# The value loads of a cached attention step, begun by ScalarE on its own DMA queue

## The chip, the cores and the metric

The kernel runs on one core of one Trainium2 chip. The metric is the device time of one execution in microseconds (us); lower is better. Before the change it is 1310.84 us, the median of three runs (1310.8 to 1311.07).

## The reference

One decode step: attention over a long cache, beside a gated feed-forward net, mixed by a gate per row. All data are float32.

```python
# x (4, 1, 512); k_cache, v_cache (4, 32, 4096, 128); wq (512, 4096); wo (4096, 512)
# w_gate, w_up (512, 1792); w_down (1792, 512); gate_w (512)
g = sigmoid((x * gate_w).sum(-1, keepdims=True))
q = (x @ wq) split into 32 heads of 128
p = softmax(einsum("bhqd,bhkd->bhqk", q, k_cache) * 128 ** -0.5)
o = einsum("bhqk,bhkd->bhqd", p, v_cache)
a = o (heads joined) @ wo
b = (gelu(x @ w_gate) * (x @ w_up)) @ w_down
out = g * a + (1 - g) * b
```

The two caches are 268 MB each, so nearly all that is moved is read once and used for very little arithmetic.

## The kernel before, in words

The 128 pairs of batch row and head are done in 32 tiles (NT). A tile holds four heads (HT) of one batch row: tile i is head group i // 4 and batch row i % 4 (`heads`, L128). Its keys lie as 128 partitions of 16384 numbers: each head takes 32 partitions, each partition 128 consecutive positions of 128 numbers, a row of 64 KB in memory. The values lie the same way. So one load of keys (K) or of values (V) is 128 rows of 64 KB, 8.39 MB.

There are two buffers for keys, K[0] and K[1], by the tile's parity, and one for values, V. At the start V holds wq, and at the end K[0] and K[1] hold the weights of the feed-forward net and wo.

What a tile passes through:

- **VectorE** (`keys`, L293): waits for the keys in memory and for the query in QB, multiplies the keys by the query in place (L303), sums over the 128 numbers (L304), then raises `k_free` (L305), which frees the key buffer. Then the maximum of the scores (L306 to L308), which is handed to ScalarE. VectorE's loop (L334) does the keys of tile i+1 and then divides tile i (`divide`, L310: L311 and L312), for which it waits for TensorE's `turn` of tile i. It runs in order: a division that waits holds the keys of tile i+2 behind it.
- **ScalarE** (`beside`, L322): copies the next query from PSUM (L235), spreads the one after (L229), computes the exponentials of the scores (`weights`, L318), waits for TensorE's values, and copies their sum from PSUM to o (L331).
- **TensorE** (loop at L267): spreads the next query (L232), sums the weights (`totals`, L238), waits for the values in V, multiplies weights by values in 64 matmul instructions (`values`, L245), and after ScalarE's copy of o turns it (`turn`, L250). The first of the turn's matmuls raises TensorE's count, which `at_tile[i]` names: from there on V is known to be free.

Nearly all loads are begun by SyncE (SP), in an order that is written out (L348 to L365): for each tile it waits until the keys of tile i are done and begins the keys of tile i+2, then waits for `at_tile[i]` and begins the values of tile i+1. At the end it begins w_gate and w_up, the values of tile 31, then w_down and wo; the last pieces of wo (L391) follow when the net's hidden row is done. All of these stand on one queue. ScalarE's own queue carries two small loads at the start, x and gate_w (L147 and L149).

After tile 30 TensorE does the two matmul groups of the net (L284); after tile 31 the output of the attention and of the net go through w_down and wo together (`project`, L411, and L466), and the result is stored.

Of the kernel before, what the change touches and what calls it, by code (L numbers as in the profile page):

```python
# [34 lines left out]
def tile_gated_mix(ctx: ExitStack, tc: tile.TileContext, x, kc, vc, wq, wo, w_gate, w_up, w_down, gate_w, out):  # L35
    nc = tc.nc
    P = 128
    B, H, S, D = kc.shape
# [3 lines left out]
    HT = 4  # L42
    PH = P // HT
    R = S // PH
    TW = R * D
    NG = H // HT
    NT = NG * B
# [34 lines left out]
    V = kv.tile([P, TW], F32, name="v")  # L82
# [25 lines left out]
    def semaphore(name):  # L108
        counters.append(ctx.enter_context(nc.semaphore(name)))
        return counters[-1]  # L110

    ctx.enter_context(tc.tile_critical(sync_engine=mybir.EngineType.SP, no_gpsimd_drain=True))
    SP = Line(nc.sync, None)
# [8 lines left out]
    def take(engine, sem, n=1):  # L122
        engine.wait_ge(sem, n).then_inc(sem, -n)  # L123

    sem_k = [semaphore(f"sem_k{s}") for s in range(2)]
    sem_v = semaphore("sem_v")

    def heads(src, i):  # L128
        g, b = divmod(i, B)
        return src[b, HT * g:HT * g + HT].rearrange("h (p r) d -> (h p) (r d)", p=PH)  # L130

    def load(dst, src, sem=None, name=None, engine=nc.sync):
        sem = sem or semaphore(name)
        engine.dma_start(dst, src).then_inc(sem, 16)  # L134
        return sem, 16

    def load_k(i):
        load(K[i % 2], heads(kc, i), sem_k[i % 2])

    def load_v(i):  # L140
        load(V, heads(vc, i), sem_v)

    HC, HW = KC // 2, TW // 2
    wq_rows = wq.rearrange("(p c) n -> p (c n)", c=KC)
# [68 lines left out]
    for s in range(2):  # L213
# [3 lines left out]
        wq_done = PE.do(u)  # L217
# [10 lines left out]
    def spread_query(pair, s):  # L228
        return nc.scalar.activation(QX, tile_of(QT, pair, s)[:, :, None].to_broadcast([P, HT, PH]), AF.Copy)  # L229
# [4 lines left out]
    def take_query(s):  # L234
        nc.scalar.activation(QB[s], qp[:, :D], AF.Copy, scale=scale).then_inc(a_to_d, 1)  # L235
# [25 lines left out]
    L1 = NT - 1  # L261
    PE.wait(have_QX, have_picks, have_zeros)
    at_tile = [(PE.sem, PE.n + i + 1) for i in range(NT)]
# [50 lines left out]
    def weights(s):  # L314
        take(nc.scalar, d_to_a)
        for h in range(HT):
            q = slice(h * PH, (h + 1) * PH)
            t = nc.scalar.activation(PM[q, :, h], SC[s][q, :], AF.Exp, bias=NM[s][q, :], scale=1.0,  # L318
                                     accum_out=RS[q, h:h + 1])
        return t  # L320

    def beside(s, following):  # L322
        take(nc.scalar, p_to_a)
        take_query(1 - s)
        if following is None:
            nc.scalar.sem_inc(a_to_p, 1)
        else:
            spread_query(following, s).then_inc(a_to_p, 1)
        weights(s).then_inc(a_to_p, 1)
        take(nc.scalar, p_to_a)  # L330
        nc.scalar.activation(o, po, AF.Copy).then_inc(a_to_p, 1)  # L331

    keys(0, got_k0)
# [6 lines left out]
    take(nc.vector, p_to_d)  # L340
    divide(NT // 2 - 1, 0).then_inc(d_to_p, 1)

    with nc.scalar.Fori(1, NT // 2) as i:
        for s in range(2):
            beside(s, i)
    beside(0, None)

    SP.wait(wq_done)  # L348
    load_v(0)
    for i in range(NT - 2):  # L350
        SP.wait((k_free, i + 1))
        load_k(i + 2)
        SP.wait(at_tile[i])
        load_v(i + 1)

    wo_rows = wo.rearrange("(p i) n -> p (i n)", i=WR)
    SP.wait((k_free, NT - 1))
    for s, a in enumerate((w_gate, w_up)):
        load(f[:, s * KC * F:(s + 1) * KC * F], a.rearrange("(p c) n -> p (c n)", c=KC), sem_up[s])
    SP.wait(at_tile[L1 - 1])  # L360
    load_v(L1)
    SP.wait((k_free, NT))
    got_down = load(down[:, :DR * DM], w_down.rearrange("(p i) n -> p (i n)", i=DR), name="got_down")
    got_wo = [load(down[:, (DR + r0) * DM:(DR + r1) * DM], wo_rows[:, r0 * DM:r1 * DM], name=f"got_wo{r0}")
# [90 lines left out]
    i = W2  # L455
# [42 lines left out]
```

## Time and profile before

| | |
|---|---|
| median of three runs | 1310.84 us |
| the profiled execution | 1310.84 us, its span 1309.1 us |
| busy: VectorE, TensorE matmul, ScalarE | 87%, 30%, 8% |
| moved from HBM | 564.67 MB, 431 GB/s over the span |
| DMA queue of SyncE (q1) | 564.67 MB |
| DMA queue of ScalarE (q10) | 0.02 MB |
| mean granted TensorE clock | 0.635 of full speed |

In rows of the profile PE is TensorE, DVE VectorE, ACT ScalarE, SP SyncE; SPq and ACTq are the sequencers that begin a DMA, and the time in such a row is that of beginning it, not of the transfer. A row of the timeline gives start, duration, engine, line, operation, what is written and read, shape and count, and in brackets how long the engine was idle before it and what ended that. "DVEq L123" there means that the engine's own sequencer stood in a wait of `take` (L122). A row of the windows gives the stretch, its length, each engine's busy time with the count of instructions, the granted clock, the share of time in which the DMA engines were busy, and GB/s.

### The profile page before, as it was taken

What the parts mean: (1) busy time and instruction counts of PE and PEld (TensorE: products, weight loads), DVE (VectorE), ACT (ScalarE), POOL (GpSimd) and SP (SyncE); (2) the same over time, 40 slices, a digit from 0 to 9 for tenths busy, and PEclk for the clock granted to TensorE, in tenths of its full rate; (3) what the DMA queues carried; (4) which work ended last, traced back from release to release, by engine and by line L of the source; (5) the groups of instructions that cost most, each with busy time, mean ns of one, the idle gap of its engine ahead of it and who ended that gap; (6) DMA issues with size and microseconds to landing.
All of it is one profiled execution on the core that took longest, in us unless ns stands there. A gap on an engine that the chain in (4) does not pass through costs nothing. (4 is left out here: it accounts for less than half of the span.)

```text
span 1309.1 us, 6991 instructions
## 1 busy us (share of the span) xinstructions
PE 389.2 (30%) x2708; PEld 134.3 (10%) x2708; DVE 1144.8 (87%) x267; ACT 108.5 (8%) x360; POOL 0.7 (0%) x6
## 2 busy tenths in 40 slices
PE   4032113333212333312333321233331133332147
PEld 1010001101001111000111100111110011110012
DVE  1999999899899989989998998989999898998950
ACT  1010000000000000000000000000000000000010
POOL 0000000000000000000000000000000000000000
PEclk9565566666566666556666655666665666665589
DMA  9999999999999999999999999999999999999998
GB/s 401 433 446 421 445 431 439 443 423 443 423 443 423 445 429 437 447 423 443 423 443 423 445 427 439 441 429 443 423 443 423 443 423 445 435 435 443 412 438 359
DMA packets 11130, 564.76 MB, mean 431 GB/s; under 512 B 1244, under 2 KB 1260, under 8 KB 1652
## 3 DMA queue, kind: packets, MB, share of 16 engines
q1 hardware_dynamic: 11108, 564.67, 99.6%
q8 instruction: 3, 0.05, 0.0%
q10 hardware_dynamic: 16, 0.02, 0.0%
q14 instruction: 3, 0.02, 0.0%
HBM read 564.67 MB, written 0.01 MB: 431 GB/s over the span
## 5 line engine op out<-in xcount | busy, mean ns | idle before, releaser
L303 DVE TENSOR_TENSOR k<-k,QB 128x16384 f32<-128x16384 f32 (+1 forms) x33 | 551.4, 16708 | 64.6 <-DVEq L123 61.9
L304 DVE TENSOR_REDUCE SC<-k 128x128 f32<-128x16384 f32 x32 | 551.0, 17220 | 4.7
L245 PE MATMUL bank<-v,PM 128*16 128x512 f32 x2048 | 291.8, 734 | 568.7 <-PEq L123 568.7
L245 PEld LDWEIGHTS bank<-v,PM 128*16 128x16 f32 x2048 | 69.0, 112 | 764.8 <-issue 764.8
L238 PE MATMUL bank<-RS,ones 128*128 128x4 f32 x64 | 17.7, 348 | 294.4 <-PEq L123 294.4
L331 ACT ACTIVATE o<-bank 128x512 f32<-128x512 f32 x31 | 18.5, 597 | 872.3 <-ACTq L123 872.3
L318 ACT ACTIVATE PM<-SC,nm 32x128 f32<-32x128 f32 x128 | 65.9, 515 | 195.4 <-ACTq L123 193.9
L238 PEld LDWEIGHTS bank<-RS,ones 128*128 128x128 f32 x64 | 15.9, 308 | 299.6 <-issue 299.6
L250 PE MATMUL bank<-pick,o 128*128 128x4 f32 x256 | 32.8, 251 | 28.7 <-PEq L123 28.7
L250 PEld LDWEIGHTS bank<-pick,o 128*128 128x128 f32 x256 | 31.0, 191 | 57.3 <-issue 57.3
L311 DVE RECIPROCAL ri<-bank 128x4 f32<-128x4 f32 x32 | 5.8, 183 | 22.0 <-DVEq L123 22.0
L318 ACT ACTIVATION_READ_ACCUMULATOR PM<-SC,nm 32x1 f32 x128 | 25.0, 195 | 0.0
L220 DVE COPY QT<-bank 128x16 f32<-128x16 f32 x8 | 0.9, 179 | 18.5 <-PE bank L216 18.5
L232 PE MATMUL bank<-ident,QX 128*128 128x128 f32 x66 | 15.4, 316 | 1.6 <-ACT QX L229 1.6
L306 DVE TENSOR_REDUCE m<-SC 128x1 f32<-128x128 f32 x32 | 9.2, 286 | 7.6 <-DVEq L123 7.6
L204 PE MATMUL bank<-v,xT 128*32 128x512 f32 x64 | 11.6, 892 | 5.8 <-DMA v<-in_A_wq 5.8
L235 ACT ACTIVATE QB<-bank 128x128 f32<-128x128 f32 x32 | 8.9, 277 | 50.3 <-ACTq L123 49.7
L312 DVE TENSOR_TENSOR OT<-bank,ri 128x4 f32 (+1 forms) x32 | 5.2, 161 | 7.5 <-DVEq L123 7.2
L307 DVE STREAM_TRANSPOSE mt<-m 128x32 f32<-128x32 f32 x32 | 6.8, 211 | 4.7
L470 DVE COPY res<-bank 128x128 f32<-128x128 f32 x1 | 0.3, 292 | 11.9 <-PE bank L466 11.9
L232 PEld LDWEIGHTS bank<-ident,QX 128*128 128x128 f32 x66 | 10.0, 191 | 2.8 <-issue 1.6
L308 DVE TENSOR_REDUCE nm<-mt 128x1 f32<-128x32 f32 x32 | 6.0, 186 | 4.8 <-DVEq L123 2.3
(57 smaller groups left out, 61.5 us busy)
## 6 DMA issues: line engine op xcount, KB each, us to landing
v<-in_A_wq SPq DMA_DIRECT2D x2, 4096.0 KB, 16.9
k<-in_A_k_cache SPq DMA_DIRECT2D x2, 4096.0 KB, 35.3
k<-in_B_w_gate SPq DMA_DIRECT2D x1, 3584.0 KB, 31.3
k<-in_B_w_up SPq DMA_DIRECT2D x1, 3584.0 KB, 39.4
k<-in_B_w_down SPq DMA_DIRECT2D x1, 3584.0 KB, 29.0
k<-in_A_wo SPq DMA_DIRECT2D x1, 2560.0 KB, 34.8
k<-in_A_wo SPq DMA_DIRECT2D x1, 2048.0 KB, 39.2
k<-in_A_wo SPq DMA_DIRECT2D x1, 1536.0 KB, 33.6
```

The costliest lines, as they stand in the source:

```text
L204: t = nc.tensor.matmul(PO[s][32 * j:32 * j + 32], xT[:, c, :], w[:, c, n0:n0 + HB * D], start=c == 0, stop=c == KC - 1)
L232: return nc.tensor.matmul(qp[:, :D], QX.rearrange("p h k -> p (h k)"), ident, start=True, stop=True)
L235: nc.scalar.activation(QB[s], qp[:, :D], AF.Copy, scale=scale).then_inc(a_to_d, 1)
L238: return nc.tensor.matmul(tot, ones, RS, start=True, stop=True)
L245: t = nc.tensor.matmul(po[32 * c:32 * c + M], p[:, j * M:(j + 1) * M], V[:, j * RJ * D:(j + 1) * RJ * D], start=j < 4, stop=j >= n - 4)
L250: return [nc.tensor.matmul(quo, o[:, j * D:(j + 1) * D], pick[:, j, :], start=j == 0, stop=j == RJ - 1) for j in range(RJ)]
L303: then(nc.vector.tensor_tensor(part, part, QB[s][:, None, :].to_broadcast([P, n, D]), op=OP.mult))
L304: then(nc.vector.tensor_reduce(SC[s], k, axis=AX.X, op=OP.add))
L306: then(nc.vector.tensor_reduce(m1, SC[s], axis=AX.X, op=OP.max))
L307: then(nc.vector.transpose(mt, m1.to_broadcast([P, 32])))
L318: t = nc.scalar.activation(PM[q, :, h], SC[s][q, :], AF.Exp, bias=NM[s][q, :], scale=1.0, accum_out=RS[q, h:h + 1])
L331: nc.scalar.activation(o, po, AF.Copy).then_inc(a_to_p, 1)
```

## The change

SyncE no longer begins values. ScalarE begins all 32 loads of values, on its own queue, with the same rows of 64 KB: V of tile 0 ahead of its loop, and V of the next tile in each `beside`, right behind the wait for TensorE's values and ahead of the copy of o. SyncE keeps keys and weights, in the order they had, with only the waits for free key buffers. The address of a value load now comes from the loop's register g, the batch row b being fixed in the code; so ScalarE's loop does four tiles in a turn (one head group) instead of two, and the last three tiles of that kind are written out.

```diff
-    def load_v(i):
-        load(V, heads(vc, i), sem_v)
-
...
-    def beside(s, following):
+    def load_values(g, b):
+        rows = vc[b, bass.ds(g * HT, HT)].rearrange("h (p r) d -> (h p) (r d)", p=PH)
+        load(V, rows, sem_v, engine=nc.scalar)
+
+    def beside(s, following, g, b):
         take(nc.scalar, p_to_a)
...
         weights(s).then_inc(a_to_p, 1)
         take(nc.scalar, p_to_a)
+        load_values(g, b)
         nc.scalar.activation(o, po, AF.Copy).then_inc(a_to_p, 1)
...
-    with nc.scalar.Fori(1, NT // 2) as i:
-        for s in range(2):
-            beside(s, i)
-    beside(0, None)
-
-    SP.wait(wq_done)
-    load_v(0)
+    load_values(0, 0)
+    with nc.scalar.Fori(0, NG - 1) as g:
+        for b in range(B):
+            beside(b % 2, 2 * g + 1 + b // 2, g + (b + 1) // B, (b + 1) % B)
+    for b in range(B - 1):
+        beside(b % 2, NT // 2 - 1 if b < 2 else None, NG - 1, b + 1)
+
     for i in range(NT - 2):
         SP.wait((k_free, i + 1))
         load_k(i + 2)
-        SP.wait(at_tile[i])
-        load_v(i + 1)
...
-    SP.wait(at_tile[L1 - 1])
-    load_v(L1)
     SP.wait((k_free, NT))
```

ScalarE in the second tile of a turn of its loop, before (QB is the query for the keys, QX the spread one, PM the weights, bank_101 the PSUM bank of the values' sum; a bracket names the semaphore that a row waits for):

```order
L235 ACTIVATE QB_69<-bank_102 128x128 [waits p_to_a]
L229 ISA
L229 ACTIVATE QX<-QT 128x128
L318 ACTIVATE PM,RS<-SC_66,nm_93 32x128 [waits d_to_a]
L318 ACTIVATE PM,RS<-SC_66,nm_93 32x128 x3
L331 ACTIVATE o<-bank_101 128x512 [waits p_to_a]
```

The same tile now:

```order
L232 ACTIVATE QB_69<-bank_102 128x128 [waits p_to_a]
L226 ISA
L226 ACTIVATE QX<-QT 128x128
L315 ACTIVATE PM,RS<-SC_66,nm_93 32x128 [waits d_to_a]
L315 ACTIVATE PM,RS<-SC_66,nm_93 32x128 x3
L134 ISA [waits p_to_a]
L134 DMA v<-in_A_v_cache 128x16384
L333 ACTIVATE o<-bank_101 128x512
```

The wait for the values has moved from the copy of o to the address arithmetic of the load, and the load's issue stands between the two.

SyncE's queue where the tiles begin, before (k_75 and k_76 are the two key buffers, v the value buffer; the semaphore pe is TensorE's count):

```order
L134 DMA k_75<-in_A_k_cache 128x8192 x2
L134 DMA k_76<-in_A_k_cache 128x16384
L134 UNCONDITIONAL_BRANCH
L134 DMA v<-in_A_v_cache 128x16384 [waits pe]
L134 DMA k_75<-in_A_k_cache 128x16384 [waits k_free]
```

SyncE's queue at the same place now:

```order
L134 DMA k_75<-in_A_k_cache 128x8192 x2
L134 DMA k_76<-in_A_k_cache 128x16384
L134 UNCONDITIONAL_BRANCH
L134 DMA k_75<-in_A_k_cache 128x16384 [waits k_free]
L134 DMA k_76<-in_A_k_cache 128x16384 [waits k_free]
```

The rows of v are gone; each load of keys is followed on this queue by the next load of keys.

SyncE's queue at the end of the tiles, before:

```order
L134 DMA k_76<-in_A_k_cache 128x16384 [waits k_free]
L134 DMA v<-in_A_v_cache 128x16384 [waits pe]
L134 DMA k_75<-in_B_w_gate 128x7168 [waits k_free]
L134 DMA k_75<-in_B_w_up 128x7168
L134 DMA v<-in_A_v_cache 128x16384 [waits pe]
L134 DMA k_76<-in_B_w_down 128x7168 [waits k_free]
L134 DMA k_76<-in_A_wo 128x5120
```

SyncE's queue at that end now:

```order
L134 DMA k_76<-in_A_k_cache 128x16384 [waits k_free]
L134 DMA k_75<-in_B_w_gate 128x7168 [waits k_free]
L134 DMA k_75<-in_B_w_up 128x7168
L134 DMA k_76<-in_B_w_down 128x7168 [waits k_free]
L134 DMA k_76<-in_A_wo 128x5120
```

The values of tile 31 no longer stand ahead of w_down and wo on this queue; they are on ScalarE's.

## The prediction

> **What bounds the kernel now.** I read the page first: busy shares, the slices of DMA, and the DMA issues with their KB and median us to landing (the last column).
>
> ```profile
> span 1309.1 us, 6991 instructions
> ...
> PE 389.2 (30%) x2708; PEld 134.3 (10%) x2708; DVE 1144.8 (87%) x267; ACT 108.5 (8%) x360; POOL 0.7 (0%) x6
> ...
> DMA  9999999999999999999999999999999999999998
> ...
> HBM read 564.67 MB, written 0.01 MB: 431 GB/s over the span
> ...
> v<-in_A_wq SPq DMA_DIRECT2D x2, 4096.0 KB, 16.9
> ...
> v<-in_A_v_cache SPq DMA_DIRECT2D x32, 28.1
> ...
> k<-in_A_k_cache SPq DMA_DIRECT2D x31, 42.1
> ```
>
> The DMA engines are at 9 tenths in 39 slices of 40; VectorE is idle 13% of the span. Then one tile in the middle, by windows:
>
> ```profile
> core 0: us, PE busy (x) PEld busy (x) DVE busy (x) ACT busy (x) POOL busy (x), PEclk, DMA share, GB/s
> 600.00:638.60 38.60, 10.74 (x76) 3.78 (x76) 35.44 (x8) 3.25 (x11) 0.00 (x0) 0.63 1.00 435
> ```
>
> In 38.60 us at a DMA share of 1.00 they move 435 GB/s, 16.8 MB: one tile of keys and one of values, 8.39 MB each (128 rows of 64 KB). So a transfer alone takes 19.3 us, and a tile two of them. Then the timeline, for the order of things within the tile:
>
> ```profile
> 600.18 0.33 SPq L134 DMA_DIRECT2D k<-in_A_k_cache  x1
> 603.89 17.23 DVE L303 TENSOR_TENSOR k<-k,QB 128x16384 f32<-128x16384 f32 x1 [2.12 <-DVEq L123]
> 621.26 17.22 DVE L304 TENSOR_REDUCE SC<-k 128x128 f32<-128x16384 f32 x1
> 623.08 8.83 PE L245 MATMUL bank<-v,PM 128*16 128x512 f32 x64 [18.76 <-PEq L123]
> 632.07 0.60 ACT L331 ACTIVATE o<-bank 128x512 f32<-128x512 f32 x1 [28.61 <-ACTq L123]
> 633.20 0.33 SPq L134 DMA_DIRECT2D v<-in_A_v_cache  x1
> 638.65 0.33 SPq L134 DMA_DIRECT2D k<-in_A_k_cache  x1
> 642.70 17.23 DVE L303 TENSOR_TENSOR k<-k,QB 128x16384 f32<-128x16384 f32 x1 [2.46 <-DVEq L123]
> 661.77 9.96 PE L245 MATMUL bank<-v,PM 128*16 128x512 f32 x64 [18.97 <-PEq L123]
> ```
>
> One queue serves K, V, K, V. The K load begun at 600.18 waits for the V load before it (values start at 623.08) and is used at 642.70. The V load begun at 633.20 waits 9 us for the rest of that K and feeds the values at 661.77. The K load begun at 638.65 comes behind V and cannot slow it. At its emptiest (633.20) the queue still holds 9 us of work, so it never runs dry. Bandwidth is the bound, and the waits of VectorE show that keys set its pace:
>
> ```profile
> DVE k L303 <- DVEq L123: 61.9, 31, 2.5
> ```
>
> That is 2.0 us a tile, so VectorE alone would do a tile in 36.6 instead of 38.6 us.
>
> **The change, part by part.**
>
> *ScalarE begins V.* It is the first thing after the wait for the values, so V is asked for at 632.1 instead of 633.2: worth nothing while the queue holds 9 us. Its issue stands in front of the copy of o (L331), which the turn, the division and the next keys wait for; ScalarE's own two issues bound it:
>
> ```profile
> 0.96 0.87 SPq L134 DMA_DIRECT2D v<-in_A_wq  x2
> 1.53 0.25 ACTq L134 DMA_DIRECT2D gs<-in_gate_w  x1
> 1.87 1.50 SPq L134 DMA_DIRECT2D k<-in_A_k_cache  x3
> 8.44 0.68 DVE L181 TENSOR_TENSOR gs<-gs,o 4x512 f32<-4x512 f32 x1 [4.48 <-DMA gs<-in_gate_w]
> 13.30 6.51 PE L204 MATMUL bank<-v,xT 128*32 128x512 f32 x32 [2.65 <-DMA v<-in_A_wq]
> ```
>
> 0.25 us here; I take 0.4 with the register work for a moving address (0 to 0.9). No wait is added: the wait for the values stood there before. The loop of four tiles a turn has fewer branches on an engine that is busy 8% of the span: nothing. V0 is begun some 2 us later, with 60 us of other loads ahead of it: nothing.
>
> *Two queues.* The same rows hold the main point. gate_w was begun on ScalarE's queue at 1.53, when 8.39 MB of wq stood on SyncE's (19.3 us). It was in use at 8.44, before even the first half of wq (13.30). So a load on the other queue does not wait its turn by time of issue; the engines take from both. The Trainium skill, page "DMA: Bandwidth & Descriptors", section "Queues, rings and completion order", says that each engine goes round robin over the queues that have work, a packet at a time; the trace agrees, by that 8.44 against 13.30.
>
> With rows of 64 KB on both sides I take equal shares (all for one or all for the other are rivals below). No bandwidth is won, but a K load begun after V now delays V. Three lengths give the new tile:
>
> - Transfers, X: 19.3 us each.
> - V's gap, g, from its landing to the first byte of the next V: values 9.4 (8.83 and 9.96 above), 0.2 to ScalarE, and begin plus landing 2.7 (wq's first half: 0.96 to 13.30 is 12.3, less 9.6 for 4.19 MB at 435 GB/s). Together 12.3.
> - D, from one V issue to the K issue that it allows. VectorE runs in order, and divides tile i before the keys of tile i+2. The last tile shows that path with VectorE waiting:
>
> ```profile
> 1251.21 0.33 SPq L134 DMA_DIRECT2D v<-in_A_v_cache  x1
> 1277.57 9.27 PE L245 MATMUL bank<-v,PM 128*16 128x512 f32 x64 [10.57 <-PEq L123]
> 1288.91 0.18 DVE L311 RECIPROCAL ri<-bank 128x4 f32<-128x4 f32 x1 [22.00 <-DVEq L123]
> 1289.24 0.16 DVE L312 TENSOR_TENSOR OT<-bank,ri 128x4 f32<-128x4 f32 x1
> ```
>
> Values end at 1286.84, the division at 1289.40: 2.6. Add 0.4 for ScalarE's issue, 0.2 to the next keys, and 34.8 for keys until K is free (603.89 to 638.65): 38.0 after the values, 37.8 after V's issue.
>
> Let V be begun T after the V before it. K was begun c = T − D ahead of this V and moved alone for c. K's remaining X − c and V then share, and V lands 2X − c after it began. The next T is g + 2X − c = g + 2X + D − T. So two successive tiles together take 2X + g + D = 38.6 + 12.3 + 37.8 = 88.7, and one takes 44.35: 5.7 us more than 38.65, all of it DMA engines without work (V's buffer in use, both K buffers full). The two tiles may differ; their sum does not.
>
> *When this begins.* The start is as before, with VectorE well behind the values:
>
> ```profile
> 90.40 1.03 PE L250 MATMUL bank<-pick,o 128*128 128x4 f32 x8 [0.90 <-PEq L123]
> 90.79 0.33 SPq L134 DMA_DIRECT2D v<-in_A_v_cache  x1
> 104.53 0.33 SPq L134 DMA_DIRECT2D k<-in_A_k_cache  x1
> ```
>
> The turn of tile 0 ends at 91.43, the keys of tile 1 at 104.53: VectorE comes to that division 13.1 us late. Served at half share from the start, K is early, VectorE no longer waits for it and gains 2.0 us a tile on the values: after 6 or 7 tiles it waits for the turn. Two or three more pass until K stands far enough ahead of V for the engines to run dry: tile 9 (5 to 12). The 22 tiles left cost 22 × 5.7 = 125 us.
>
> *The end.* Now the last weights set it (the first row is of the chain that ended last):
>
> ```profile
> 1269.00 36.47 DMA k<-in_A_wo
> ```
>
> ```profile
> 1293.68 2.75 PE L411 MATMUL bank<-k,ow 128*4 128x512 f32 x20 [0.38 <-DVE ow L437]
> 1296.93 1.90 PE L411 MATMUL bank<-k,ow 128*4 128x512 f32 x16 [0.49 <-DMA k<-in_A_wo]
> 1300.54 1.89 PE L411 MATMUL bank<-k,ow 128*4 128x512 f32 x12 [1.71 <-DMA k<-in_A_wo]
> 1303.00 1.04 PE L411 MATMUL bank<-k,ow 128*4 128x512 f32 x8 [0.57 <-DMA k<-in_A_wo]
> 1304.39 0.64 PE L466 MATMUL bank<-k,o 128*32 128x128 f32 x16 [0.35 <-DMA k<-in_A_wo]
> 1306.01 0.29 DVE L470 COPY res<-bank 128x128 f32<-128x128 f32 x1 [11.91 <-PE bank L466]
> ```
>
> Values 31 start 1277.57 and the span ends 31.5 later, 3.1 of that waits for weights: the chain alone is 28.4, and the last bytes land at 1305.5, 3.6 before the end. The 27 us of w_down and wo that stood behind V31 now move beside it; I take 11 us still to come when V31 lands (8 to 19). The end is then 28.4 + 0.5 − 11 = 18 after the last byte instead of 3.6: 14 more (6 to 17).
>
> Sum: 125 + 14 = 139 on a profiled run of 1310.84 (its span 1309.1, and 1.7 outside), which is also the median of the runs: **1450 us**, 11% slower. Its own bounds: 19 to 26 tiles by 4.9 to 6.1 (values 8.8 to 10, overhead 1.5 to 3, issue 0 to 0.9), with the end: 1410 to 1487.
>
> **Rivals.**
>
> *Served in order of issue, or in long bursts (0.10): no change.* If a queue kept the engines for a whole load of eight rows, the order would be K, V, K, V as now, and 1.1 us earlier on a queue that holds 9 is worth 0: 1309 to 1312 us. For it: engines already full. Against it: gate_w got through a queue of 19.3 us in under 7. The same page, "Issuing engines are not separate DMA queues", says that issuing from several engines saves only the issue time; by that rule the sum would be this, 1310.8.
>
> *Faster (0.04).* 564.67 MB at 435 GB/s are 1298 us; with some 2 at the start (the first issue is at 0.96), 3.6 at the end and 1.7 outside the span, 1305. It needs engines that stay full with two queues, and the weights still the last to land.
>
> *A late lock, or V first (0.06): 1312 to 1410.* If the rows of a new load stand behind several that the engines have already taken from the other queue, K's lead over V grows later: dry from tile 20, 11 × 5.7 + 14 gives 1387; from tile 28, 1342. If V were always served first, its loop would be g + X = 31.6 us, under 38.65: keys stay the bound, as now.
>
> *K always first (0.04).* Then V waits for all of K from the first tiles on, and VectorE's 13.1 us are gone at once: 31 × 5.7 + 14 = 191, 1502 us. The early gate_w load speaks against it: it got past wq.
>
> **How the numbers follow.** Forecast 0.76. Beyond 0.2% (2.6 us, about what a measurement of this kernel can tell): faster 0.04, same 0.10, slower 0.76 + 0.06 + 0.04 = 0.86. The range 1360 to 1490 holds the forecast with its bounds and part of the late locks; it leaves out no change, faster, K first and the rest, together near 0.2.
>
> **What would show it.** DMA share under 0.9 in the middle, in holes of up to 10 us while values run; V's time to landing from 28 up to 30 to 38, K's from 42 down to 20 to 38; VectorE no longer waiting at L303 for K but at L311 for the turn; tiles of 44 us, perhaps long and short in turn, after a first stretch at 38.6; some 28 us from the start of values 31 to the end. It is wrong if the slices stay at 9 (then queues keep order of issue), or if the rate with both queues active is not 435 GB/s.

## The result, and the profile after

| | before | after |
|---|---|---|
| median, four runs each on one chip | 1310.95 us | 1472.74 us (1472.56 to 1475.21) |
| ratio | | 1.124 (95% interval 1.122 to 1.125) |
| span of the profiled run | 1309.1 us | 1471.0 us |

The forecast was 1450 us, 1360 to 1490. The page of the changed kernel: busy shares, the slices of DMA and the two queues; the last two lines, of its view of DMAs, are the loads' median times to landing.

```profile
span 1471.0 us, 7023 instructions
...
PE 387.4 (26%) x2708; PEld 135.7 (9%) x2708; DVE 1146.0 (78%) x267; ACT 106.5 (7%) x360; POOL 0.7 (0%) x6
...
DMA  9999999898989979798897989989799897979977
...
q1 hardware_dynamic: 6500, 296.23, 47.8%
q10 hardware_dynamic: 4624, 268.45, 42.2%
...
v<-in_A_v_cache ACTq DMA_DIRECT2D x32, 32.7
...
k<-in_A_k_cache SPq DMA_DIRECT2D x31, 31.8
```

Every engine's work is as before (VectorE 1146.0 us against 1144.8); the DMA engines have lost their unbroken nines from the eighth slice on. Keys land 10 us sooner than before, values 5 us later. Who waits has changed as well (us in total, times, longest):

```profile
DVE ri L308 <- DVEq L123: 224.3, 27, 30.5
...
DVE k L300 <- DVEq L123: 13.4, 32, 1.3
```

VectorE waited for keys (61.9 us); now it waits 27 times at the division, for the turn of values that come late. The timeline of two tiles in the middle:

```profile
703.11 88.98 SPq L134 DMA_DIRECT2D k<-in_A_k_cache  x3
...
705.70 0.34 ACTq L134 DMA_DIRECT2D v<-in_A_v_cache  x1
...
708.01 0.18 DVE L308 RECIPROCAL ri<-bank 128x4 f32<-128x4 f32 x1 [3.85 <-DVEq L123]
...
743.64 0.29 DVE L303 TENSOR_REDUCE m<-SC 128x1 f32<-128x128 f32 x1 [0.24 <-DVEq L123]
...
744.39 8.92 PE L242 MATMUL bank<-v,PM 128*16 128x512 f32 x64 [32.58 <-PEq L123]
...
753.60 0.34 ACTq L134 DMA_DIRECT2D v<-in_A_v_cache  x1
...
755.90 0.18 DVE L308 RECIPROCAL ri<-bank 128x4 f32<-128x4 f32 x1 [11.28 <-DVEq L123]
...
785.00 9.10 PE L242 MATMUL bank<-v,PM 128*16 128x512 f32 x64 [25.28 <-PEq L123]
...
794.38 0.34 ACTq L134 DMA_DIRECT2D v<-in_A_v_cache  x1
```

Values are begun at 705.70, 753.60 and 794.38: tiles of 47.9 and 40.8 us, 88.7 together. Keys are begun at 703.11 and, when VectorE has freed their buffer, just ahead of 743.64 (SyncE's three issues stand merged in the first row). The same stretch by windows:

```profile
714.20:733.50 19.30, 0.00 (x0) 0.00 (x0) 19.15 (x2) 0.00 (x0) 0.00 (x0) 0.50 1.00 435
744.00:753.60 9.60, 8.92 (x64) 2.10 (x64) 0.40 (x2) 0.00 (x0) 0.00 (x0) 0.78 1.09 437
756.00:776.00 20.00, 0.64 (x3) 0.50 (x2) 19.11 (x4) 2.58 (x10) 0.00 (x0) 0.56 0.97 419
782.00:791.00 9.00, 6.00 (x40) 1.51 (x44) 9.00 (x1) 0.00 (x0) 0.00 (x0) 0.60 0.02 7
```

A window counts a row where it starts, and the rows start in rounds of 16, 2.42 us apart. The first window holds eight whole rounds with both queues at work: 435 GB/s, the rate of before. The prediction had named another rate with both queues active as a sign that it is wrong; that sign did not come. The third window holds eight rounds too, in 20 us, hence 419; keys alone move 437. In the last window the values are being multiplied, both key buffers are full, and the engines move 7 GB/s: that is where the time is lost. The queues in the first of those windows (packets, MB, share of 16 engines):

```profile
q10 hardware_dynamic: 64, 4.19, 50.2%
q1 hardware_dynamic: 64, 4.19, 50.1%
```

64 rows of values against 64 of keys: equal shares, as assumed. Round by round the 16 rows are 11 of values and 5 of keys (714 to 716), then 5 and 11 (716 to 718.5), then 11 and 5 again (719 to 721): the queues change after every single row.

Where the 161.9 us lie is read off ScalarE's issues of V1, V4, V30 and V31:

```profile
94.36 0.37 ACTq L134 DMA_DIRECT2D v<-in_A_v_cache  x1
...
217.28 0.34 ACTq L134 DMA_DIRECT2D v<-in_A_v_cache  x1
...
1374.53 0.34 ACTq L134 DMA_DIRECT2D v<-in_A_v_cache  x1
...
1412.71 0.37 ACTq L134 DMA_DIRECT2D v<-in_A_v_cache  x1
```

Before, V1 stood at 90.79 and V31 at 1251.21, 30 tiles of 38.68. So: 3.6 us until V1; 6.9 over three tiles to V4; then 26 tiles of 44.51, 5.83 more than before, 151.5; −0.5 in the last tile; and 58.3 instead of 57.9 us from V31 to the end, 0.4. Together 161.9.

### The profile page after: what moved, and what is told of

Same layout as the page of the kernel before. It is cut to its first block, busy times and chain, and to the rows that moved or that the text cites. A ratio compares the mean times of both kernels' runs of the same rounds, so it can differ in the third digit from the quotient of the medians.

```text
span 1471.0 us, 7023 instructions
## 1 busy us (share of the span) xinstructions
PE 387.4 (26%) x2708; PEld 135.7 (9%) x2708; DVE 1146.0 (78%) x267; ACT 106.5 (7%) x360; POOL 0.7 (0%) x6
## 5 line engine op out<-in xcount | busy, mean ns | idle before, releaser
L226 ACT ACTIVATE QX<-QT 128x128 f32 (+1 forms) x32 | 9.8, 308 | 2.4 <-DVE QT L217 1.6
(57 smaller groups left out, 48.3 us busy)
```

## The experiments

The theory is that of the prediction: the engines take a row from each queue in turn, so a key load begun near a value load delays it; VectorE must divide tile i before the keys of tile i+2, so late values in turn set when keys are begun; and the tile settles at a length at which the engines run dry. The rivals: the cost lies in ScalarE (the issue, the moving address, the longer loop), or in two queues as such. Each run is one time beside one of the kernel before on the same chip (1310.79 to 1310.88 us).

### The loop alone

Against the changed kernel; only ScalarE's longer loop stays.

```diff
-        load_values(g, b)
...
-    load_values(0, 0)
...
+    SP.wait(wq_done)
+    load_v(0)
     for i in range(NT - 2):
         SP.wait((k_free, i + 1))
         load_k(i + 2)
+        SP.wait(at_tile[i])
+        load_v(i + 1)
...
```

> ScalarE's loop of four tiles a turn, but SyncE begins the values again, as before. Theory (two queues share the DMA engines row by row, so a key load delays a value load, and keys then wait for the division of values that come late): the loop is no part of it, 1309 to 1314 us. Rival (the cost lies in ScalarE's instruction stream: longer loop, address arithmetic): some of the 162 us is still there, 1330 us or more.

1311.33 us. The loop of four tiles costs nothing that one run can show.

### Keys on ScalarE's queue too

```diff
+        take(nc.scalar, d_to_a)
+        if more:
+            load_keys(s, g + (b + 1) // B, (b + 1) % B)
         weights(s).then_inc(a_to_p, 1)
         take(nc.scalar, p_to_a)
         load_values(g, b)
...
-        load_k(i + 2)
```

> ScalarE begins the keys of all tiles from tile 2 on too, so keys and values stand on one queue again, but on ScalarE's; values are asked for as early as in the changed kernel. Theory: in order of issue again, 1309 to 1318 us, DMA share 0.99 or more in the middle. Rival (ScalarE's issue of loads is what costs): 60 loads with moving addresses instead of 31, 1473 us or more.

1325.38 us: 147 less than the changed kernel although ScalarE begins twice as many loads, but 7 above the expected range. A window of the middle:

```profile
700.00:738.60 38.60, 10.54 (x76) 3.76 (x76) 35.23 (x8) 3.25 (x11) 0.00 (x0) 0.63 1.00 435
```

In the middle a tile is the 38.60 us at 435 GB/s of before. The missing part lies where two queues still meet. At the start V0 shares with the first keys on SyncE's queue, and VectorE's second half of tile 0 begins late:

```profile
56.70 8.69 DVE L300 TENSOR_TENSOR k<-k,QB 128x8192 f32<-128x8192 f32 x1 [15.48 <-DMA k<-in_A_k_cache]
```

Before, it began at 42.25. At the end V30 and V31 share with the weights. By the issues of values, 6.4 us of the 14 lie ahead of V1 (97.22 against 90.79) and 9.4 in the tile from V30 to V31; the 29 tiles between are 1.9 us shorter than before. So ScalarE's issue is refuted as the cause.

### Keys in quarters: 16 KB against 64 KB

```diff
-        load(K[i % 2], heads(kc, i), sem_k[i % 2])
+        rows, n = heads(kc, i), TW // 4
+        for a in range(4):
+            load(K[i % 2][:, a * n:(a + 1) * n], rows[:, a * n:(a + 1) * n], sem_k[i % 2])
...
-            take(nc.vector, sem_k[s], 16)
+            take(nc.vector, sem_k[s], 64)
```

> Values as in the changed kernel, rows of 64 KB; each key load is four loads of a quarter of the columns, rows of 16 KB. Theory, turns by row: values get 64 of 80 KB moved, land 19.3 x 1.25 = 24 us after they start, their loop is 24 + 12 = 36 us, under 38.65: 1310 to 1325 us. Rival (equal shares by bytes or time whatever the rows): 1473 us.

1332.9 us, 8 above the expected range and 140 below the changed kernel, with the same two queues. The queues from 725 to 735 us, with both at work:

```profile
q10 hardware_dynamic: 63, 4.13, 95.2%
q1 hardware_dynamic: 72, 0.98, 23.1%
```

12 packets of this window are under 512 B and carry no row; 0.98 MB are 60 rows of keys beside 63 of values, but a quarter of the bytes. The turns go by row, and a queue's share of bandwidth by the size of its rows. Of the 22 us over before, 5.9 lie ahead of V1, as in the run above, 11.8 in the 29 tiles to V30 and 4.4 behind it.

### Values in quarters

```diff
-        load(V, rows, sem_v, engine=nc.scalar)
+        n = TW // 4
+        for a in range(4):
+            load(V[:, a * n:(a + 1) * n], rows[:, a * n:(a + 1) * n], sem_v, engine=nc.scalar)
...
-        take(nc.tensor, sem_v, 16)
+        take(nc.tensor, sem_v, 64)
```

> Keys in rows of 64 KB; each value load is four loads of a quarter of the columns, rows of 16 KB. Theory, turns by row: values get a fifth while keys are there, keys pass first and the lock starts at once: 31 tiles x 5.8 = 180 us over before, 1490 to 1510 us. Equal shares by bytes: 1473 us.

1556.26 us: the right way, 46 past the range. VectorE waits at the division from the first tile on:

```profile
DVE ri L308 <- DVEq L123: 313.9, 32, 39.7
```

Two tiles take 92 us instead of 88.7 (copies of o 51.1 and 41.0 us apart). Part of that is the issue, which stands ahead of the copy of o:

```profile
713.43 1.86 ACTq L134 DMA_DIRECT2D v<-in_A_v_cache  x4
715.34 0.60 ACT L335 ACTIVATE o<-bank 128x512 f32<-128x512 f32 x1 [45.08 <-issue]
```

1.9 us for four loads against 0.4 for one (705.70 to 706.09): 1.6 more on the mean of twelve tiles. Most of the other 1.8 us lies with TensorE, whose `turn` now follows the values after 3.0 us of idling and not after 1.4:

```profile
716.08 1.84 PE L247 MATMUL bank<-pick,o 128*128 128x4 f32 x8 [3.00 <-PEq L123]
```

That turn takes 1.84 us at a granted clock of 0.50; in the changed kernel it took 1.02 (at 754.73) at 1.00. The values before it take 9.87 us at 0.71, against 8.92 and 9.10 at 0.79 and 0.77. That is 0.8 us in each of the two, and with the issue 3.2 of the 3.4. Why the clock is lower is not shown.

### Both in quarters

The two edits above together.

> Keys and values both as four loads of quarter rows, 16 KB each, on the two queues. Theory, turns by row: equal shares again, 1460 to 1485 us. If smaller rows or more loads as such made a difference, it would stand away from the changed kernel's 1473 us on one side.

1510.59 us, 26 past the range. Two tiles again take 92 us (44.4 and 47.7), by the same dearer issue and the same slower TensorE (on the mean of twelve tiles issue 1.5, turn 0.6 and values 0.5 us more, together 2.7 of 3.4); the lock begins at tile 6, against 5 in the changed kernel. From 720 to 735 us, 3.28 MB of keys and 3.15 of values are moved. Equal rows give equal shares and the loss; rows of 16 KB as such do not help.

### Keys in halves

The key edit with two loads of half rows, 32 KB, in place of four.

> Key loads in two halves, rows of 32 KB; values in rows of 64 KB. Theory, turns by row: values get two thirds, between the whole and the quartered keys, 1360 to 1410 us. Equal shares by bytes: 1473 us.

1415.32 us, 5 above the range: between whole keys (1472.74) and quartered ones (1332.9). Two tiles take 85.3 us, locked from tile 7.

### Keys in quarters on one queue

The key edit above, made in the kernel before.

> The kernel before (one queue) with each key load from tile 1 on as four loads of quarter rows of 16 KB: what the pieces cost without a second queue. Theory: order of issue holds, nothing else changes, 1310 to 1318 us. If quartered keys with two queues were 22 us over before because of the small rows, it shows here, 1325 to 1335 us.

1315.25 us. Of the 22 us that quartered keys with two queues stand over before, 4 are the pieces. With the 5.9 ahead of V1 that makes 10; the other 12 stay open.

### More work on VectorE, 2.3 us a tile

```diff
+        then(nc.vector.tensor_reduce(SC[s][:, :16], k[:, :16], axis=AX.X, op=OP.add))
         then(nc.vector.tensor_reduce(SC[s], k, axis=AX.X, op=OP.add))
```

> The changed kernel with 2.3 us more work on VectorE in each tile: the sums of 16 of the 128 positions of each partition are done once more, ahead of all of them (2048 of 16384 numbers by 17.22 us). VectorE alone then needs 39.0 us a tile instead of 36.7, more than the 38.65 of the transfers. Theory: keys are no longer asked for faster than the queue can serve both, VectorE never catches up with the values, no lock: FASTER than the changed kernel, 1315 to 1345 us. Rival (two queues cost bandwidth, or ScalarE's issue costs): 1473 us or more.

1334.6 us. The changed kernel with 73 us more work on VectorE is 138 us **faster**. The added instruction by lines, and a tile by windows:

```profile
L301 DVE TENSOR_REDUCE SC<-k 128x16 f32<-128x2048 f32 x32 | 73.2, 2286 | 4.7
```

```profile
700.00:739.00 39.00, 10.43 (x76) 3.77 (x76) 37.42 (x9) 3.26 (x11) 0.00 (x0) 0.63 1.00 430
```

The engines are full again, and no division waits for the turn but the last:

```profile
DVE ri L309 <- DVEq L123: 11.2, 1, 11.2
```

Neither ScalarE's issue nor a cost of two queues as such can be undone by work on VectorE; the pace at which keys are asked for can. In the kernel before the same work costs little:

> The same added 2.3 us a tile in the kernel before. VectorE becomes the bound at 39.0 us a tile: 32 x 0.4 = 13 us, 1318 to 1330 us; the price of the added work without the second queue.

1319.11 us. Of the 15.5 us between the two runs, 7.9 lie ahead of V1 (99.73 against 91.87), where V0 still shares with the first keys; the rest is not taken apart.

### Half as much: 1.2 us a tile

```diff
+        then(nc.vector.tensor_reduce(SC[s][:, :8], k[:, :8], axis=AX.X, op=OP.add))
```

> The changed kernel with 1.2 us more work on VectorE in each tile (8 of 128 positions summed twice), so 37.9 us a tile, still under the 38.65 of the transfers. Theory: VectorE still catches up with the values, only later, and each locked tile is 0.6 us longer, since the added work lies in the path from value issue to key issue: 1440 to 1475 us, with a later start of the lock. If added VectorE work helped for a reason other than the pace of the keys, it would help by half of what 2.3 us did, about 1400 us.

1461.96 us. VectorE takes 38.0 us a tile, still under 38.65: the lock comes, at tile 11 instead of 5. So half the work does not buy half the gain; there is an edge, somewhere between 38.0 and 39.0 us of VectorE a tile, and the transfers' 38.65 lies in between.

### Keys that wait for the values

```diff
+            if j == 0:
+                t.then_inc(v_read, 1)
...
         SP.wait((k_free, i + 1))
+        SP.wait((v_read, i + 1))
         load_k(i + 2)
```

> The changed kernel, but SyncE begins the keys of tile i+2 only when the first value matmul of tile i has run, so never while that value load is under way. Theory: the keys then run alone for about 9 us while the values are multiplied, and share the rest with the next value load; a tile is g + 2X - 9 = 12 + 38.6 - 9 = 41 to 42 us, from the first tile to the last and without long and short in turn: 1370 to 1410 us. A rival in which two queues cost a fixed share of bandwidth would leave it at 1473 us or, with the added wait, above.

1455.55 us, above the range. Its tiles are 43.1 us on the mean (copies of o from 97.27 to 1432.56, 31 tiles), in no two-tile pattern:

```profile
736.82 8.98 PE L243 MATMUL bank<-v,PM 128*16 128x512 f32 x64 [11.29 <-PEq L123]
...
738.76 43.59 SPq L135 DMA_DIRECT2D k<-in_A_k_cache  x2
...
746.08 0.34 ACTq L135 DMA_DIRECT2D v<-in_A_v_cache  x1
...
789.90 0.34 ACTq L135 DMA_DIRECT2D v<-in_A_v_cache  x1
```

The keys are begun 1.9 us after the first value matmul starts, so their lead over V is 7.3 us and not 9. With 7.3 the formula of the prediction, g + 2X − c, gives 12.3 + 38.6 − 7.3 = 43.6; measured 43.8. On the mean of tiles 1 to 29 the lead is 7.50, the formula gives 43.4, and 43.24 was measured. The formula held, the lead was mis-sized.

## Why the prediction was right, and where its terms were off

**Order and shares: right.** Equal shares by row (64 against 64 rows), and the quarters move the time both ways as turns by row demand. This is the round robin that the Trainium skill gives on the page "DMA: Bandwidth & Descriptors", section "Queues, rings and completion order"; the page says that a packet is typically some 9 to 17 descriptors, while here the turn changed after every single row of 64 KB. The rival "served in order of issue" is refuted by the two packet counts. That issuing from a second engine wins no bandwidth (the same page of the Trainium skill, "Issuing engines are not separate DMA queues") agrees with 435 GB/s before and after; that the time would then stay the same did not follow.

**The length of a locked tile: right.** X, g and D gave 88.7 us for two tiles, 44.35 for one. The trace has 88.68 from 705.70 to 794.38, and 44.51 on the mean of 26. D was 37.8 and is 37.9 (705.70 to 743.6). The formula holds for three leads: c = 2.6 gives 48.3 (measured 47.9), c = 10.0 gives 40.9 (40.8), c = 7.3 gives 43.6 (43.8). Its agreement to 0.1 us is in part luck, since two terms were off and nearly cancel. In the tile begun at 705.70 the first row of V starts 3.9 us after the issue (709.61) and the last one ends at 743.96, 0.4 ahead of the value matmuls: begin and landing take 4.3 us, not 2.7. The rows of V then take 34.4 us, and 27.3 in the next tile, not the 36.0 and 28.6 of 2X − c.

**When it begins: too late, the term that missed.** I let VectorE gain 2.0 us a tile on the values, from a lead of 13.1, and put the lock at tile 9. The copy of o and the freed keys, at tile 0 and at tile 4:

```profile
94.78 0.60 ACT L333 ACTIVATE o<-bank 128x512 f32<-128x512 f32 x1 [10.91 <-ACTq L123]
...
116.59 0.33 SPq L134 DMA_DIRECT2D k<-in_A_k_cache  x1
...
262.50 0.60 ACT L333 ACTIVATE o<-bank 128x512 f32<-128x512 f32 x1 [32.16 <-ACTq L123]
263.92 0.33 SPq L134 DMA_DIRECT2D k<-in_A_k_cache  x1
```

21.8 us between them at tile 0, 1.4 at tile 4: 5.1 lost a tile. The step failed in keeping values at 38.65 a tile while VectorE ran at 36.8: keys begun every 36.8 us take 19.3 of them, 17.5 are left, and a value load needs 19.3 × 36.8 / 17.5 = 40.6 us. So VectorE gains at least 3.8 a tile. The start also differed, where the prediction had put V0 at nothing: V0, sharing with the first keys, made VectorE later (80.55 instead of 68.48 for its first freed buffer), and the lead began at 20, not 13. The added work on VectorE bears the reckoning out in kind: at 38.0 us a tile it gives a loss of 39.2 − 38.0 = 1.2, measured 1.8 over tiles 0 to 9; at 39.0 none, and none was measured. Instead of 22 tiles × 5.7 = 125, the tiles cost 26 × 5.83 = 151.5, and 10.5 before that.

**The end: mis-sized.** I added 14 us (6 to 17); from V31 on it is 0.4:

```profile
1444.53 8.72 PE L242 MATMUL bank<-v,PM 128*16 128x512 f32 x64 [19.39 <-PEq L123]
...
1460.10 6.20 PE L409 MATMUL bank<-k,ow 128*4 128x512 f32 x56 [0.38 <-DVE ow L435]
```

The chain now runs without waits for weights, as said, and takes 26.5 us from 1444.53 to the end, not 28.4. V31 took 31.8 us from issue to use instead of 26.4, and the rest 5 us less than before (31.5): the two nearly cancel. I had reckoned that only 11 us of weights were left behind it; the last piece, begun at about 1426.8 and landing 35.6 us later, shows 18, so the end is some 8.6 us after the last byte, 5 more than before. This miss and the late start stood against each other: until V31 the kernel lost 161.5 us where 125 were put down, at the end 0.4 where 14 were. That the total came within 23 us is luck in this part.

**ScalarE's issue: right.** 0.4 us ahead of the copy of o, no cost of its own; the loop none.

## What to carry to other kernels

One queue is also an order: putting two streams that share a bandwidth limit on two queues lets the stream that is asked for sooner, or in larger rows, push the other back, even where no byte is added. Ask then which of the two frees the other's buffers, and add up one round of that loop (the transfer, with what shares with it, and the work until the next issue) against the bandwidth's own time for a round. If two queues are wanted, the row sizes set the shares, as the runs with keys in quarters and halves show.

## What the runs showed of the hardware

Turns went by row, not by bytes: 64 rows against 64 where both had 64 KB, 63 rows of 64 KB beside 60 of 16 KB in 10 us, a share of 4 to 1. Four loads in a row hold ScalarE for 1.9 us where one takes 0.34, and TensorE's `turn` behind them ran at a granted clock of 0.50 instead of 1.00. And a busy engine can be a useful brake: 2.3 us more work a tile on VectorE took 138 us off the changed kernel, 1.2 us only 11.
